# Window attention and a softplus FFN: the order of every engine planned inside the kernel by due times, and the low halves of the weights moved from GpSimd to VectorE

## The chip, the cores and the metric

The kernel runs on one core of one Trainium2 chip. The metric is device time in microseconds (us); lower is better. The engines are TensorE (PE in the profile, PEld its weight loads), VectorE (DVE), ScalarE (ACT), GpSimd (POOL) and SyncE (SP), which issues the DMAs. Each engine runs its own instruction list in order; semaphores tie the lists together.

## The reference

Attention over a window of 64 keys, for 8 batches, 8 heads, 576 tokens and head size 64, and then a feed-forward network (FFN) with a softplus between its two products.

```python
scores = scale * q @ k.T                     # 0 <= row - column < 64 only
attn = exp(scores - max); attn = attn / (sum(attn) + 1e-9)
x = (attn @ v) as 4608 tokens x 512
h = x @ w_in                                 # 512 x 2048
g = maximum(h, 0) + log1p(exp(-abs(h)))
out = g @ w_out                              # 2048 x 512
```

The weights reach the kernel as 64-bit words of double-precision numbers. The kernel makes 32-bit floats of them itself.

## The kernel before

The 4608 tokens are cut into 12 blocks `g` of `TB` = 384. The attention of a block is done in four units `hp` of two heads each (`attention(g, hp)`), so there are 48 units. A unit loads q, k and v, forms scores on PE, takes scaled minima (L258, DVE), exponentials (L295, ACT), scales by the sums (L300, L301, L303, DVE), transposes the result and multiplies by v. It leaves its part of x as two tiles, a rounded high part and the rest (`x0` by ACT, `x1` by DVE, L374 and L375). Blocks 0 and 1 (`by_pe`) transpose on PE (L310) and multiply in 32 bits (L369); block 2 still forms its scores from quarters of the array (`quad`, L268); blocks 3 to 11 use split operands (L281), and blocks 2 to 11 transpose by DMA and multiply in bf16 (L410).

The FFN of a block has 16 steps `f`, one for each 128 columns of the hidden layer; there are 192 steps. `ffn_up(g, f)` (below: U) makes 12 matmuls of 384 columns (L435), then Abs, Exp and Ln on ACT (L439 to L441), the sum on DVE (L443), a rounded copy `g0` (L445, on ACT for blocks 0 and 1 and for odd `f`, else on DVE) and the rest `g1` (L446, DVE). `ffn_down(g, f)` (D) makes 9 matmuls of 512 columns (L456) into three banks of sums. The passes run 8 steps of block 0, 16 of block 1, the other 8 of block 0, and then the blocks 2 to 11 in order. The sums of the first pass are copied out (L475), spilled to DRAM and added later (L473).

`load_w(f)` fetches one of 16 slices of both weight matrices (1 MB of words) and turns it into floats: ACT takes absolute values (L174), DVE does four bit operations (L175 to L178), ACT copies a rounded high part (L181), and GpSimd subtracts it for the low part (L182). Words and half-made floats pass through a few staging tiles (`raws`, `ws`, `raw`, `wh`), which share memory with other things.

The order comes from a list of events with positions written by hand: U of step n at 2n + 0.5, D at 2n + `DOWN` (so D of a step follows the U two steps later), weight slice f at `CONVERT[f]`, and each stage of a unit at `BASE`, `PACE`, `SH`, `SHP` and `STG`. From position `PE_ORDERED_FROM` on (about step 50) PE keeps this order; before that, and on all other engines throughout, the framework's own planner orders the instructions by its timeline.

Of the kernel before, what the change touches and what calls it, by code (L numbers as in the profile page):

```python
# [8 lines left out]
F32 = mybir.dt.float32  # L9
# [12 lines left out]
NCH = TB // CH + 1  # L22

SPLIT = 8
DOWN = 5.5
CONVERT = (-104, -98, -93, -88, -6, -3, 0, 3, 6, 8, 11, 13, 16, 18, 21, 24)
BASE = (-100, -10, 24)
PACE = (5, 4, 7)
STG0 = (-4.5, 0.5, 1, 2, 3, 4, 7, 8)
STG = (-13, -5.9, -5, 0, 1, 2, 3, 4, 5, 6, 7, 7.1, 12, 14, 16, 17)  # L30
SH, SHP = -12, 8
PE_ORDERED_FROM = 100
BY_PE, QUADS = 2, 3
MANUAL = {mybir.EngineType.PE}

ZERO_HIGH = 2.0**-15


@with_exitstack
def window_attention_softplus_ffn(  # L40
# [10 lines left out]

# [21 lines left out]
    ORDER = list(range(0, NT // TB, NPER))[:2]  # L73
    ORDER += [b for b in range(NT // TB) if b not in ORDER]
    QSCALE = -1.0 / float(D) ** 0.5

# [5 lines left out]
    late = ctx.enter_context(tc.tile_pool(name="late", bufs=1))  # L82
# [5 lines left out]
    nc.scalar.preload_act_table_set("natural_log_exp_and_others")  # L88

    NE = NF // 2
    w_first = [[cpool.tile([P, NE, DM], F32R, name=f"w{m}{i}") for i in range(2)] for m in range(2)]
    w_last = {}

    def spare(k, shape, dtype, name):
        return late.tile(shape, dtype, name=name, tag=f"spare{k}")

    def weight(m, i, f):

        if f < NE:
            return w_first[m][i][:, f, :]
        k = (f - NE) // 4
        if (m, i, k) not in w_last:
            w_last[m, i, k] = spare(4 * k + 2 * m + i, [P, 4, DM], F32R, f"w{m}{i}{k}")
        return w_last[m, i, k][:, f % 4, :]


    W = CH + P
# [6 lines left out]
    nc.gpsimd.memset(k_two[:, :, 0:CH], 0.0)  # L116

    v13 = cpool.tile([P, NCH, 2, 2, D], BF16, name="v13")
    nc.gpsimd.memset(v13, 0.0)
    v_first = [att.tile([P, 2, NJ, P], F32, name="v_first", tag=n) for n in ("nat", "tr")]  # L120
    for t in v_first:
        nc.vector.memset(t[0:CH, 0, 0, :], 0.0)

    FAR = BIG / QSCALE
    wide, wide_c, wide_b = [cpool.tile([P, W], BF16, name=n) for n in ("wide", "wide_c", "wide_b")]
    nc.gpsimd.memset(wide, 0.0)
    nc.gpsimd.affine_select(
        out=wide, in_=wide, pattern=[[1, W]], compare_op=ALU.is_gt, fill=FAR, base=0, channel_multiplier=-1  # L130
    )
    nc.gpsimd.affine_select(
        out=wide, in_=wide, pattern=[[-1, W]], compare_op=ALU.is_ge, fill=FAR, base=CH, channel_multiplier=1
    )


    mask_q = att.tile([P, 3, P], BF16, name="mask_q", tag="k0")
    mask, mask_c, mask_b = [mask_q[:, i, :] for i in range(3)]
    for m in (mask_c, mask, mask_b):
        nc.gpsimd.tensor_copy(m[0:CH, :], wide[0:CH, 0:P])  # L140
        nc.gpsimd.tensor_copy(m[CH:P, :], wide[CH:P, CH:W])
    nc.gpsimd.memset(mask_c[0:CH, 0:CH], FAR)
    nc.gpsimd.memset(mask_b[CH:P, 0:CH], FAR)
    nc.gpsimd.tensor_copy(wide_c, wide)
    nc.gpsimd.memset(wide_c[:, 0:CH], FAR)
    nc.gpsimd.tensor_copy(wide_b, wide)
    nc.gpsimd.memset(wide_b[CH:P, 0:P], FAR)
    masks = {True: (mask, mask_c, mask_b), False: (wide, wide_c, wide_b)}
    ident = att.tile([P, P], F32, name="ident", tag="xf")
    make_identity(nc, ident)  # L150

    mm, tp = nc.tensor.matmul, nc.tensor.transpose

    def load_w(f):


        if f < NE + 4:
            k = (0, 4, 2, 6)[f % 4] if f < NE else (4, 6)[f % 2]
            parts = [(spare(k, [P, 2, DM], w_words.dtype, "raws"), spare(k + 1, [P, 2, DM], F32, "ws"), 0, 2)]
        else:  # L160
            parts = [
                (
                    ff.tile([P, 1, DM], w_words.dtype, name="raw"),
                    att.tile([P, 1, DM], F32, name="wh", tag=("v_in", "v12")[m]),
                    m, m + 1,
                )
                for m in range(2)
            ]
        for raw, w, m0, m1 in parts:
            nc.sync.dma_start(raw, w_words[f][:, m0:m1, :])  # L170
            words = raw.bitcast(U32).rearrange("p m (n two) -> p two m n", two=2)
            low, high = words[:, 0, :, :], words[:, 1, :, :]
            wb = w.bitcast(U32)
            nc.scalar.activation(w, high.bitcast(F32), AF.Abs)  # L174
            nc.vector.tensor_scalar(w, w, ZERO_HIGH, None, ALU.max)  # L175
            nc.vector.tensor_scalar(wb, wb, 3, 0x3FFFFFF8, ALU.logical_shift_left, ALU.bitwise_and)  # L176
            nc.vector.scalar_tensor_tensor(wb, high, 0xC0000000, wb, ALU.bitwise_and, ALU.bitwise_or)  # L177
            nc.vector.scalar_tensor_tensor(wb, low, 29, wb, ALU.logical_shift_right, ALU.bitwise_or)  # L178
            for m in range(m0, m1):
                hi, lo = [weight(m, i, f) for i in range(2)]  # L180
                nc.scalar.copy(hi, w[:, m - m0, :])  # L181
                nc.gpsimd.tensor_tensor(lo, w[:, m - m0, :], hi.bitcast(F32), ALU.subtract)  # L182


    xs = {}
    taken_ps = [0]

    def attention(g, hp):
# [3 lines left out]
        by_pe = g < BY_PE  # L192
        quad = g < QUADS
        odd0 = g == 0 and hp % 2 == 1

        def bank():
            if not odd0:
                return ps_a.tile([P, 512], F32, name="ps_a")

            taken_ps[0] += 1  # L200
            return ps_o.tile([P, 512], F32, name=f"ps_o{taken_ps[0] % NJ}")

        heads = [slice(0, D), slice(D, P)]
# [353 lines left out]
```

## Time and profile before

| | |
|---|---|
| median of 3 runs | 1028.54 us (1028.44 to 1029.22) |
| the profiled execution's own time | 1027.8 us |
| its span, first to last instruction | 1026.0 us |
| PE, PEld | 971.5 us (95%), 861.0 us (84%) |
| DVE, ACT, POOL | 796.1 us (78%), 734.9 us (72%), 58.9 us (6%) |
| DMA | 117.38 MB, mean 114 GB/s |

The rows of 40 slices cut the span into stretches of 25.65 us, each digit the busy share in tenths. A group's row gives its line, engine and operation, the busy time, the mean of one instruction, and the idle time ahead of it with what ended most of it. A row of the timeline gives start, length (a merged row's first start to last end), engine, line and count, and in square brackets the idle time before it. The start and end of matmuls are partly modelled.

### The profile page before, as it was taken

How to read it: one execution, taken by the hardware profiler on the slowest of the kernel's cores; microseconds unless marked ns; L12 is line 12 of the kernel's file. 1: busy time of each engine (PE TensorE's matmuls, PEld its weight loads, DVE VectorE, ACT ScalarE, POOL GpSimd, SP SyncE). 2: the span in 40 equal slices, each digit the busy share in tenths (PEclk: the TensorE clock that was granted, in tenths of full speed). 3: DMA queues.
4: the chain of work that ended last, by engine and by line, in shares of the span. 5: the costliest groups of instructions: out<-in, count | busy, mean ns of one | idle time of the engine just before them, and what ended most of it. 6: DMA issues, size and time to landing. Idle time of an engine off the chain costs nothing.

```text
span 1026.0 us, 17028 instructions
## 1 busy us (share of the span) xinstructions
PE 971.5 (95%) x6128; PEld 861.0 (84%) x6128; DVE 796.1 (78%) x1777; ACT 734.9 (72%) x1697; POOL 58.9 (6%) x55
## 2 busy tenths in 40 slices
PE   2668979999999999999999999999999999999998
PEld 2447758888988999898998899899989999888997
DVE  6999585588987888888888878878878887874332
ACT  5556585688877787788778778778778878865443
POOL 4265010000000000000000000000000000000000
PEclk9999989999999999999999999999999999999999
DMA  9653151475553445444444444535645635521000
GB/s 347 214 167 104 40 161 37 83 188 122 142 123 96 113 119 128 114 113 128 120 113 119 128 100 116 145 85 119 157 83 114 165 83 113 133 49 32 31 1 31
DMA packets 201749, 117.38 MB, mean 114 GB/s; under 512 B 130496, under 2 KB 193728, under 8 KB 200128
## 3 DMA queue, kind: packets, MB, share of 16 engines
q1 hardware_dynamic: 201664, 116.29, 43.6%
q8 instruction: 48, 0.79, 0.3%
q14 instruction: 37, 0.30, 0.1%
HBM read 74.58 MB, written 10.22 MB: 83 GB/s over the span
## 4 chain that ended last, share of the span: by engine, by line
PE 84%; DVE 10%; DMA 3%; issue 2%; ACT 1%; SPq 0%; ACTq 0%; DVEq 0%
PE ps_h L435 37%; PE ps_o L456 37%; PE ps_a L410 5%; PE ps_a L281 5%; DVE ws L177 1%; DVE ws L178 1%; DVE st L258 1%; DVE ws L176 1%; DVE st L303 1%; DVE ws L175 1%; DMA raws<-in_w_words_dram 1%; DMA tr<-nat 1%; DVE u L443 1%; DMA raw<-in_w_words_dram 0%; PE ps_a L268 0%
## 5 line engine op out<-in xcount | busy, mean ns | idle before, releaser
L435 PE MATMUL ps_h<-x,w 128*128 128x384 f32 x2304 | 448.5, 342 | 15.3 <-DVE x L375 9.1
L456 PE MATMUL ps_o<-w,g 128*128 128x512 f32 x1728 | 434.5, 394 | 0.5 <-DVE g L446 0.5
L435 PEld LDWEIGHTS ps_h<-x,w 128*128 128x128 f32 x2304 | 405.6, 190 | 31.0 <-DVE x L375 10.8
L456 PEld LDWEIGHTS ps_o<-w,g 128*128 128x128 f32 x1728 | 318.2, 188 | 58.8 <-DVE g L446 1.3
L439 ACT ACTIVATE u<-ps_h 128x384 f32<-128x384 f32 x192 | 94.0, 490 | 129.2 <-PE ps_h L435 126.5
L443 DVE SCALAR_TENSOR_TENSOR u<-ps_h,u 128x384 f32<-128x384 f32 x192 | 106.2, 553 | 75.6 <-ACT u L441 74.3
L295 ACT ACTIVATE st<-st,mn 128x128 f32<-128x128 f32 x288 | 112.1, 390 | 18.4 <-DVE mn L258 14.5
L446 DVE TENSOR_TENSOR g<-u,g 128x384 fp32r<-128x384 f32 x192 | 109.1, 568 | 13.0 <-ACT g L445 11.1
L440 ACT ACTIVATE u<-u 128x384 f32<-128x384 f32 x192 | 100.9, 526 | 3.3
L441 ACT ACTIVATE u<-u 128x384 f32<-128x384 f32 x192 | 100.3, 522 | 4.1
L258 DVE CUSTOM_DVE_ANT_0 st<-ps_a,wide 128x192 f32<-128x192 f32 x176 | 57.0, 351 | 44.5 <-PE ps_a L281 44.4
L410 PEld LDWEIGHTS <-v 128*128 128x128 bf16 x1136 | 56.5, 98 | 21.6 <-issue 20.3
L445 ACT CAST g<-u 128x384 fp32r<-128x384 f32 x112 | 57.0, 509 | 21.1 <-DVE u L443 20.3
L410 PE MATMUL ps_a<-tr,v 128*128 128x128 bf16 (+1 forms) x1136 | 70.2, 211 | 0.2 <-DMA tr<-nat 0.2
L281 PE MATMUL ps_a<-k,q_hl 128*128 128x192 f32 x432 | 69.1, 281 | 0.0
L281 PEld LDWEIGHTS ps_a<-k,q_hl 128*128 128x128 f32 x432 | 59.8, 191 | 3.1
L326 ACT CAST nat<-st 128x768 bf16<-128x768 f32 x40 | 33.2, 830 | 40.0 <-DVE st L324 39.9
L295 ACT ACTIVATION_READ_ACCUMULATOR st<-st,mn 128x1 f32 x288 | 53.9, 187 | 0.0
L415 ACT COPY xf<-ps_a 64x384 f32<-64x384 f32 x80 | 38.1, 477 | 20.2 <-PE ps_a L410 18.9
L303 DVE TENSOR_TENSOR st<-st,sm 128x768 f32<-128x768 f32 x48 | 50.2, 1045 | 1.2
L345 DVE TENSOR_TENSOR v_in<-v_in,v 128x896 f32<-128x896 f32 x40 | 43.5, 1087 | 5.8 <-ACT v L344 5.7
L348 DVE TENSOR_TENSOR v<-v_in,v 64x896 bf16<-64x896 f32 x40 | 43.6, 1089 | 5.1 <-PE ps_a L410 2.1
(81 smaller groups left out, 860.6 us busy)
## 6 DMA issues: line engine op xcount, KB each, us to landing
v_in<-in_v_dram SPq DMA_DIRECT2D x80, 224.0 KB, 3.6
k_in<-in_kT_dram SPq DMA_DIRECT2D x72, 224.0 KB, 3.8
q_in<-in_qT_dram SPq DMA_DIRECT2D x72, 192.0 KB, 4.1
raws<-in_w_words_dram SPq DMA_DIRECT2D x12, 1024.0 KB, 5.7
out_dram<-raw SPq DMA_DIRECT2D x12, 512.0 KB, 2.8
raw<-in_w_words_dram SPq DMA_DIRECT2D x8, 512.0 KB, 5.3
out_dram<-raw SPq DMA_DIRECT2D x12, 256.0 KB, 2.6
q_two<-in_qT_dram SPq DMA_DIRECT2D x12, 192.0 KB, 3.5
```

Source lines behind the costliest of these rows:

```text
L258: nc.vector.tensor_tensor_reduce(st[:, hh, j, :], scores, m, QSCALE, 3.0e38, ALU.add, ALU.min, mn[:, hh, j : j + 1])
L281: mm(spv[:, hh, :], q_hl[:, hh, js], part[:, hh, kc], start=(hh == 0 and i == 0), stop=(hh == 1 and i == 1), skip_group_check=True,)
L295: nc.scalar.activation(sv[:, i, 0:P], sv[:, i, 0:P], AF.Exp, bias=mn[:, hh, j : j + 1], scale=-1.0, accum_out=sm[:, i : i + 1])
L303: nc.vector.tensor_tensor(pn, pn, sm.unsqueeze(2).to_broadcast([P, 2 * NJ, P]), ALU.mult)
L410: mm(av[:, osl], (v13 if s else v12)[:, c, hh, :, :], src, start=(i == 0), stop=(i == len(passes) - 1), skip_group_check=True,)
L435: mm(hv, weight(0, a, f)[:, c * P : (c + 1) * P], x[b][c], start=(i_mm == 0), stop=(i_mm == 3 * NC - 1))
L439: nc.scalar.activation(u, hv, AF.Abs)
L440: nc.scalar.activation(u, u, AF.Exp, scale=-1.0)
L441: nc.scalar.activation(u, u, AF.Ln, bias=1.0)
L443: nc.vector.scalar_tensor_tensor(gf, hv, 0.0, u, ALU.max, ALU.add)
L446: nc.vector.tensor_tensor(gt[1], gf, gt[0].bitcast(F32), ALU.subtract)
L456: mm(ops[g][j], gt[a][:, js], weight(1, b, f), start=(first and i == 0), stop=(last and i == 2),)
```

## The change

The events, their positions and the framework's ordering go. The kernel first writes its work as a list of `Op`s: an engine, a cost in us, the ops that it depends on, and the buffers that it opens or uses. `arrange` then runs these through a small model: on each engine, among the ops that could start, the one with the earliest due time is taken; an op that opens a buffer waits until the buffer's former users are done; a result reaches the next engine `RESULT` later. Due times come from `dues`: U of step n at the time given for it, D at `DOWN` later, a unit's x ahead of its block's first step by `AHEAD` and `APART`, and everything before these by its cost and latency, times `STRETCH`. Four rounds are planned, each with the U times of the last; the one that ends first in the model is emitted, and all engines keep that order (`manual_schedule()` without a list of engines). A DMA's op starts at most `EARLY` before it is due.

In the kernel's work itself: the low part of the weights is subtracted by DVE over both matrices at once, and GpSimd's part goes; each slice has a place of its own (`w{f}`), into which its words land by one DMA and which then takes the floats; copies of block 0 and 1's transposes are all on ACT; six small mask copies go from GpSimd to DVE; q and k have four places instead of two in blocks 0 and 1, and the k of the first two units is issued by ACT; v of blocks 0 and 1 is loaded for all heads at once; the score tiles have three places, the transposed ones two; unit 2 of block 0 uses the banks of U.

```diff
-DOWN = 5.5
-CONVERT = (-104, -98, -93, -88, -6, -3, 0, 3, 6, 8, 11, 13, 16, 18, 21, 24)
...
+DOWN = 6.3
+AHEAD = (1, 1, 8, 8)
+APART = (4, 6, 18, 19)
+STRETCH = 1.4
+EARLY = 30
+RESULT = {"PE": 0.25, "DVE": 0.12, "ACT": 0.15, "POOL": 0.2, "SP": 2.0}
...
+def arrange(ops, rings):
...
+    free = {"PE": 0.0, "DVE": 0.8, "ACT": 2.1, "POOL": 0.8, "SP": 0.8}
...
+    while len(order) < len(ops):
...
+                at = max(ready_at[id(o)], o.due - EARLY if e == "SP" else 0.0)
...
+            t = max(free[e], min(at for at, _ in could))
+            o = min((o for at, o in could if at <= t + 1e-9), key=lambda o: o.due)
+            if best is None or t < best[0]:
+                best = (t, o)
...
-                hi, lo = [weight(m, i, f) for i in range(2)]
-                nc.scalar.copy(hi, w[:, m - m0, :])
-                nc.gpsimd.tensor_tensor(lo, w[:, m - m0, :], hi.bitcast(F32), ALU.subtract)
...
+    w_raw = [buf(cpool, [P, 2, DM], w_words.dtype, "raw", tag=f"w{f}") for f in range(NF)]
+    w_all = [buf(cpool, [P, 2, 2, DM], F32R, "w", tag=f"w{f}") for f in range(NF)]
...
+        a = add("SP", 0.45, lambda: nc.sync.dma_start(raw(), w_words[f]), opens=[raw], nbytes=1024 * 1024, name=f"load{f}")
+        a = add("ACT", 1.05, lambda: nc.scalar.activation(work(), word(1).bitcast(F32), AF.Abs), deps=[a], opens=[work], uses=[raw], name=f"abs{f}")
+        a = add("DVE", 0.6, lambda: ts(work(), work(), ZERO_HIGH, None, ALU.max), deps=[a], uses=[work], name=f"c1.{f}")
...
+        h = add("ACT", 1.05, lambda: nc.scalar.copy(weights(0, f), work()), deps=[a], opens=[w], uses=[work], name=f"hi{f}")
+        lo = add("DVE", 1.13, lambda: tt(weights(1, f), work(), weights(0, f).bitcast(F32), ALU.subtract),
+                 deps=[h], uses=[work, w], name=f"lo{f}")
...
+                if skip:
+                    nc.gpsimd.memset(qk(1)[:, 0:CH], 0.0)
+                by.dma_start(qk(1)[:, skip:], kT[c0 : c0 + P, t0 - CH + skip : t0 + TB])
...
+        a = add("PE", 2.09, up, deps=[o for hp in range(NP) for o in x_ops[g, hp]] + converted[f] + ups[-1:], opens=[hps],
+                uses=[b for i in range(2) for b in x[i]] + [w_all[f]], name=f"U{g}.{f}")
+        s = add("ACT", 1.21, soft, deps=[a], opens=[u], uses=[hps], name=f"soft{g}.{f}")
+        m = add("DVE", 0.47, lambda: stt(u(), hps()[:, :TB], 0.0, u(), ALU.max, ALU.add), deps=[s], uses=[hps, u], name=f"m{g}.{f}")
+        h = add("ACT" if by_act else "DVE", 0.41 if by_act else 0.28,
...
+        lo = add("DVE", 0.47, lambda: tt(gt[1](), u(), gt[0]().bitcast(F32), ALU.subtract), deps=[h], opens=[gt[1]],
+                 uses=[u, gt[0]], name=f"g1.{g}.{f}")
...
+        d = add("PE", 2.06, down, deps=[h, lo, *downs[-1:]], opens=acc if first else [], uses=[*gt, w_all[f]] + ([] if first else acc), name=f"D{g}.{f}")
...
+        for n, t in enumerate(times):
+            ups[n].due = t
+            downs[n].due = t + DOWN
...
+            x1.due = firsts[g] - AHEAD[min(g, 3)] - (NP - 1 - hp) * APART[min(g, 3)]
...
-    for at, emit in events:
-        if at < PE_ORDERED_FROM:
-            emit()
-    with tc.manual_schedule(engines=MANUAL):
...
+    for _ in range(ROUNDS):
...
+        dues(times)
+        order = arrange(ops, rings)
+        end = max(o.end for o in order)
+        if best is None or end < best[0]:
+            best = (end, [(o, o.start) for o in order])
+        times = [o.start for o in ups]
+    with tc.manual_schedule():
+        setup()
+        for o, at in best[1]:
+            o.fn()
```

More of the change, by code (lines that the diff above doesn't have):

```diff
@@ new lines, with __init__, __call__ @@
+EARLY = 30
+ZERO_HIGH = 2.0**-15
+RESULT = {"PE": 0.25, "DVE": 0.12, "ACT": 0.15, "POOL": 0.2, "SP": 2.0}
+BYTES_PER_US = 260e3
+SMALL = 400e3
+class Ring:
+    def __init__(self, n):
+        self.n, self.taken, self.held, self.made = n, [], [], 0
+class Buf:
+    def __init__(self, ring, make):
+        self.ring, self.make, self.tile, self.users = ring, make, None, []
+    def __call__(self):
+        if self.tile is None:
+            self.tile = self.make()
+        return self.tile
+class Op:
+    def __init__(self, eng, cost, fn, deps=(), opens=(), uses=(), nbytes=0, name=""):
+        self.eng, self.cost, self.fn, self.name, self.nbytes = eng, cost, fn, name, nbytes
+        self.deps, self.opens = [d for d in deps if d is not None], list(opens)
+        self.due = self.start = self.end = 0.0
+        self.later = []
+        for d in self.deps:
+            d.later.append(self)
+        for b in [*uses, *opens]:
+            b.users.append(self)
@@ new lines, in attention, with turn @@
+            v_now, lv = v_loads[g]
+            pt = buf(att, [P, 2, TB], F32, "pt", tag=("q_hl", "k1")[hp % 2])
+            cp, t = [], None
+            for hh in range(2):
+                pp = bank()
+                def turn(hh=hh, pp=pp):
+                    for j in range(NJ):
+                        tp(pp()[:, j * P : (j + 1) * P], sv()[:, hh * NJ + j, 0:P], ident)
+                t = add("PE", 0.7, turn, deps=[nrm, t], opens=[pp] if hh else [pp, pt], uses=[st, two["xf"]], name=f"T{tag}")
+                cp.append(add("ACT", 0.4, lambda hh=hh, pp=pp: nc.scalar.copy(pt()[:, hh, :], pp()[:, :TB]),
+                              deps=[t], uses=[pp, pt], name=f"cp{tag}"))
@@ L505, in window_attention_softplus_ffn, with dues @@
-    events.sort(key=lambda e: e[0])
-    for at, emit in events:
-        if at < PE_ORDERED_FROM:
-            emit()
-    with tc.manual_schedule(engines=MANUAL):
-        for at, emit in events:
-            if at >= PE_ORDERED_FROM:
-                emit()
+            attention(g, hp)
+    for n, step in enumerate(steps):
+        ffn(n, *step)
+    def dues(times):
+        for o in ops:
+            o.due = 1e9
+        for n, t in enumerate(times):
+            ups[n].due = t
+            downs[n].due = t + DOWN
+        for n, o in stores:
+            o.due = times[n] + DOWN + 4
+        firsts = {}
+        for n, (g, f, first, last) in enumerate(steps):
+            firsts.setdefault(g, times[n])
+        for (g, hp), (x0, x1) in x_ops.items():
+            x1.due = firsts[g] - AHEAD[min(g, 3)] - (NP - 1 - hp) * APART[min(g, 3)]
+        for o in reversed(topo):
+            for s in o.later:
+                o.due = min(o.due, s.due - STRETCH * (o.cost + RESULT[o.eng]) if s not in downs_set else s.due - o.cost - RESULT[o.eng])
@@ new lines, in window_attention_softplus_ffn @@
+    topo, seen = [], {}
+    for o in ops:
+        seen[id(o)] = len(o.deps)
+    ready = [o for o in ops if not o.deps]
+    while ready:
+        o = ready.pop()
+        topo.append(o)
+        for s in o.later:
+            seen[id(s)] -= 1
+            if not seen[id(s)]:
+                ready.append(s)
+    downs_set = set(downs)
+    times, t = [], 20.0
+    for n, (g, f, first, last) in enumerate(steps):
+        times.append(t)
+        t += 4.2 + (0.6 if g >= 2 else 1.0)
+    best = None
```

735 lines of the change are left out of this document (406 added, 329 removed).

## The prediction

> **What bounds the kernel now.** I read the page's parts 1, 2 and 4 first, then a table of windows, then the timeline of PE and DVE in the first 175 us, and last the waits behind the FFN's chain.
>
> ```profile
> span 1026.0 us, 17028 instructions
> PE   2668979999999999999999999999999999999998
> GB/s 347 214 167 104 40 161 37 83 188 122 142 123 96 113 119 128 114 113 128 120 113 119 128 100 116 145 85 119 157 83 114 165 83 113 133 49 32 31 1 31
> PE 84%; DVE 10%; DMA 3%; issue 2%; ACT 1%; SPq 0%; ACTq 0%; DVEq 0%
> ```
>
> The chain that ended last is PE's. After some seven slices of 25.65 us PE has no idle tenth. The windows say where the border lies:
>
> ```profile
> 30.00:60.00 30.00, 17.41 (x116) 12.61 (x116) 30.00 (x58) 15.85 (x44) 12.72 (x8) 1.00 0.57 194
> 60.00:90.00 30.00, 23.16 (x136) 18.50 (x136) 29.88 (x50) 19.54 (x47) 14.65 (x10) 1.00 0.48 161
> 90.00:126.00 36.00, 32.43 (x234) 27.22 (x234) 26.54 (x60) 22.08 (x61) 12.26 (x8) 1.00 0.12 36
> 126.00:175.00 49.00, 40.59 (x268) 34.83 (x267) 35.42 (x90) 33.81 (x90) 6.14 (x4) 0.93 0.38 112
> 360.85:439.38 78.53, 78.53 (x497) 70.77 (x497) 65.82 (x151) 61.58 (x142) 0.00 (x0) 1.00 0.46 118
> ```
>
> The columns are the stretch, its length, and the busy time of PE, PEld, DVE, ACT and POOL. From 30 to 90 us DVE has no gap. In the last row, one period of the steady part (16 steps and 4 units: 16 x 21 + 4 x 40 = 496 matmuls), PE has none. The price of a step without attention comes from the chain near the end, in order of time:
>
> ```profile
> 927.94 2.10 PE ps_h L435 x12
> 930.05 2.08 PE ps_o L456 x9
> 932.13 2.10 PE ps_h L435 x12
> ```
>
> A step costs PE 932.13 - 927.94 = 4.19 us, and a unit (78.53 - 16 x 4.19)/4 = 2.87 us. All 192 steps are 804.5 us, 36 units of blocks 3 to 11 103.3 us; for block 2's four units I estimate 2.3 us each and for the eight by PE 2.45 us (the rows below). That is 937 us of work at full pace. The kernel needs 1021 us to its last matmul, so about 84 us go to waits and to slow matmuls, and the steady part holds none of them. So the change can gain only in the first 175 us, and it can lose anywhere in the 850 us behind, where there is nothing to gain.
>
> **What the first 175 us are spent on.**
>
> ```profile
> L182 POOL TENSOR_TENSOR w<-ws,w x24: 1273/1720/2327, 16.5 to 99.0; 128x512 fp32r<-128x512 f32 x24
> 124.98 0.69 DVE L475 COPY raw<-ps_o 128x512 f32<-128x512 f32 x1 [1.73 <-PE ps_o L456]
>   DVE x L375: 19.8, 7
> ```
>
> The first row: the subtractions of 12 slices of weights (two rows each) are done by 100 us. The second is the copy of the sums after the first 8 steps: these end at 125 us and need 8 slices. The third, from the list of what L435 waited for: U waited 19.8 us for x. DVE, full as it is, converts weights that are wanted 50 us later while x is late. A planner that goes by due times would turn that around.
>
> **The DVE account to step 8.** Rows of single instructions (minimum/median/maximum in ns):
>
> ```profile
> L175 DVE TENSOR_SCALAR ws<-ws x12: 647/680/1560, 9.5 to 88.9; 128x1024 f32<-128x1024 f32 x12
> L176 DVE TENSOR_SCALAR ws<-ws x12: 676/694/1757, 10.2 to 90.3; 128x1024 uint32<-128x1024 uint32 x12
> L177 DVE SCALAR_TENSOR_TENSOR ws<-raws,ws x12: 1209/1215/2169, 10.9 to 92.5; 128x1024 uint32<-128x1024 uint32 x12
> L178 DVE SCALAR_TENSOR_TENSOR ws<-raws,ws x12: 1209/1212/2290, 13.3 to 95.8; 128x1024 uint32<-128x1024 uint32 x12
> L303 DVE TENSOR_TENSOR st<-st,sm x48: 940/958/2047, 19.3 to 916.2; 128x768 f32<-128x768 f32 x48
> L446 DVE TENSOR_TENSOR g<-u,g x192: 540/551/1648, 83.3 to 1018.1; 128x384 fp32r<-128x384 f32 x192
> 39.02 0.28 DVE L258 CUSTOM_DVE_ANT_0 st<-ps_o,mask_q 128x128 f32<-128x128 f32 x1
> 39.23 0.28 DVE L258 CUSTOM_DVE_ANT_0 st<-ps_o,mask_q 128x128 f32<-128x128 f32 x1
> L375 DVE TENSOR_TENSOR x<-ps_a,x x6: 515/545/558, 31.9 to 128.3; 128x384 fp32r<-128x384 f32 x6
> ```
>
> A slice's four operations are 0.68 + 0.69 + 1.22 + 1.21 = 3.80 us. The moved subtraction (1024 columns of floats, two inputs) has no row on DVE. Its bounds are L303's 0.96 us for 768 columns and L178's maximum of 2.29 us; I take L178's median, 1.21 us, the same width. So a slice costs DVE 5.0 us. What speaks for the move is the maxima: during POOL's subtractions L176 took up to 1.76 us instead of 0.69, L446 1.65 instead of 0.55. With POOL silent these delays go, up to about 1.1 us for each of its 32 subtractions, and 16 x 1.21 = 19 us come in their place. So DVE's sum changes little either way; the account below uses prices without delays.
>
> To the end of step 8, DVE must do 8 slices (40 us), 8 units (six minima at 39.23 - 39.02 = 0.21 us, two small ones of 0.35 together, 0.96 and 0.55: 3.1 us each, 25 us) and 8 FFN steps at 2 x 0.55 (9 us): 74 us. The start:
>
> ```profile
> 3.77 1.56 PE L268 MATMUL ps_a<-k_two,q_two 64*64 64x128 f32 x24 [3.77 <-POOL wide L132]
> 8.34 1.12 ACT L174 ACTIVATE ws<-raws 128x1024 f32<-128x1024 f32 x1 [6.31 <-DMA raws<-in_w_words_dram]
> 15.30 7.55 SPq L170 DMA_DIRECT2D raws<-in_w_words_dram  x2
> ```
>
> The words land at 8.34 us and DVE has weight work from 9.5 us. Until then it can do at most two units' minima (2.5 us) and the six mask copies that leave POOL (about 1 us, hidden there). 9.5 + 74 - 2.5 = 81, a closing D 2 us, and I allow 4 us for gaps: step 8 ends at 87 us instead of 125. The words don't bound this: at the 347 and 214 GB/s of the page's first two columns 1 MB lands each 3 to 5 us, and with a place per slice of weights SP need not sit 7.55 us in two issues (the third row), behind which v waited. The two k issues moved to ACT fall in its idle 6.3 us. The memsets of k stand behind POOL's setup, so the first scores come some 1 to 4 us later than now (3.77 us, the first row); DVE's weight work from 9.5 us covers that, and without this cover it comes out of the allowance. V's 20 loads made 5 only free SP.
>
> **ACT's account to step 8.**
>
> ```profile
> L181 ACT CAST w<-ws x24: 602/618/625, 15.7 to 97.9; 128x512 fp32r<-128x512 f32 x24
> L295 ACT ACTIVATE st<-st,mn x27: 385/386/402, 12.4 to 57.6; 128x128 f32<-128x128 f32 x27
> L311 ACT COPY pt<-ps_a 128x384 f32<-128x384 f32 x6 | 2.8, 475 | 7.3 <-PE ps_a L310 7.3
> ```
>
> A slice costs ACT 1.12 + 2 x 0.62 = 2.4 us, a unit six exponentials of 0.39, two transposes' copies (one came from DVE) and one of x at 0.48: 3.8 us. With some 2.1 us for a step's four operations (rows below) that is 66 us for 8 of each, under DVE's 74.
>
> **The sum.** The state of the kernel before at 175 us, U and D:
>
> ```profile
> L435 PE MATMUL ps_h<-x,w x216: 331/337/689, 29.8 to 174.1; 128*128 128x384 f32 x108
> L456 PE MATMUL ps_o<-w,g x139: 387/393/500, 83.8 to 175.0; 128*128 128x512 f32 x139
> ```
>
> From step 8, PE has 184 steps (771 us), 36 units (103 us), block 2's units (9 us), less the U of the next step, done by then: 881 us. Check on the kernel before: some 18 U (12 matmuls each) and 15.6 D (9 each) are begun by 175 us, and the same prices for the rest give 846 us, so 1021, where its matmuls end. 87 + 881 = 968. The kernel before had step 8 at 125 us, 125 + 881 = 1006, so it lost 15 us more on the way to block 3 (8.4 us of them idle in the row 126:175). In the new kernel that may be anything from 0 to 15; I take 8. Then the steady part, the largest unknown.
>
> **The steady part's new waits.** The FFN chain after a U, near the end where nothing is in its way:
>
> ```profile
> 1004.67 2.27 PE L435 MATMUL ps_h<-x,w 128*128 128x384 f32 x12
> 1006.98 0.49 ACT L439 ACTIVATE u<-ps_h 128x384 f32<-128x384 f32 x1 [2.58 <-PE ps_h L435]
> 1008.61 0.56 DVE L443 SCALAR_TENSOR_TENSOR u<-ps_h,u 128x384 f32<-128x384 f32 x1 [2.50 <-ACT u L441]
> 1009.21 0.51 ACT L445 CAST g<-u 128x384 fp32r<-128x384 f32 x1 [0.63 <-DVE u L443]
> 1009.75 0.56 DVE L446 TENSOR_TENSOR g<-u,g 128x384 fp32r<-128x384 f32 x1 [0.58 <-ACT g L445]
> 1015.15 6.32 PE L456 MATMUL ps_o<-w,g 128*128 128x512 f32 x27
> ```
>
> From U's start to `g1` it takes 1010.31 - 1004.67 = 5.64 us. The planner's costs and latencies make it 2.09 + 0.25 + 1.21 + 0.15 + 0.47 + 0.12 + 0.41 + 0.15 + 0.47 + 0.12 = 5.44 us with the copy on ACT, and 5.04 us with it on DVE: 0.2 and 0.6 us too little, 0.4 on average, mostly because it prices the three ACT operations at 1.21 where 1008.61 - 1006.98 = 1.63 us pass. The old order set D two U's later, 1015.15 - 1004.67 = 10.5 us after the start of its own U. With `DOWN` = 6.3 the due times put it after the next U, at 6.3 us: room of 0.6 us, on an ACT that is busy 61.6 and a DVE that is busy 65.8 of 78.5 us. Where the model sees D late it sends another U first, which brings the old room back. Where it sees it just in time, the chip is late, and behind a late D the whole of PE waits. Bounds: 0 (the model always finds room), and 0.4 us in each of some 160 steps with attention beside them, 64 us. I take a wait of 0.25 us in a third of them, 14 us, nearer to zero since after each wait the other engines have caught up. At the very end the last D comes 2.09 us after its U instead of 6.3, so PE waits 5.64 - 4.19 = 1.5 us.
>
> 968 + 8 + 14 + 1.5 to the last matmul, and 4.5 us of copies and stores as now (1026.0 - 1021.5): a span of 996 us. The profiled execution took 1.8 us more than its span (1027.8), and the median of the runs shown 0.7 more than that: 998 us.
>
> **A slower PE at the start.** Here the same 12 matmuls early and later:
>
> ```profile
> 36.84 1.54 PE L268 MATMUL ps_o<-k_two,q_two 64*64 64x128 f32 x12
> 110.55 0.87 PE L268 MATMUL ps_a<-k_two,q_two 64*64 64x128 f32 x12
> ```
>
> PE works at 0.56 of its pace until about 80 us although the granted clock reads 1.00. If that stays so to step 8, a step costs 4.19 x 1.77 = 7.4 us and a unit 4.3: from a first U at 28 us (four units on ACT, 15 us, behind the first q and k, and a slice) 8 x 7.4 + 4 x 4.3 = 76 us, step 8 at 104. I take DVE's 87, since PE would then be busy without gaps. [...]
>
> **Rivals.** (1) Slower: the FFN chain is late for D in nearly every step. At 64 us instead of 14 the span is 1046, the time 1048. It turns slower from (14 + 1026 - 996)/160 = 0.28 us a step. For it: the model's missing 0.4 us. Against it: the model's own way out, a U ahead. (2) Cold PE binds the first 8 steps, step 8 at 104: 1015 us. For it the rows above, against it DVE's longer account in the gaps. (3) The planned order does no more than the old one in the first part, since DVE's sum is about the same: step 8 at 125, the old 15 us after it and no new waits: 1028. Against it: 12 slices done by 100 us and U waiting for x. (4) No new waits in the steady part: 984 us; a case of my forecast's lower end.
>
> **How the numbers follow.** Forecast with (4): 0.64; its own range 976 to 1012. (2) 0.15; (3) or a like cancelling 0.04; slower by (1) 0.17. Some 0.2% (2 us) is what a measurement here can tell. Faster is 0.64 + 0.15 = 0.79, same 0.04, slower 0.17. The range runs from 976 (0.06 lie below) to 1034, short of (1)'s full price, with 0.12 above.
>
> **What would show it.** Right: POOL's L182 gone, a DVE subtraction of about 1.2 us, L175 to L178 without maxima over 1.4 us; the first full U near 28 us, the spill's copies near 87 instead of 125; PE's idle time behind block 2 about 15 us, ended by `g1`. Wrong: waits of D over 44 us in sum, spread over all blocks, or matmuls at half pace up to 100 us.

## The result and the profile after

The changed kernel takes 995.53 us (median of 4 runs, 993.75 to 995.96) against 1028.49 us before: a ratio of 0.9676, 95% interval 0.9659 to 0.9693. The forecast was 998.0 us, with a range from 976 to 1034. First the page of the changed kernel: its span, the rows of PE, of the granted clock and of the DMA rate over 40 slices, and the chain that ended last.

```profile
span 991.9 us, 16876 instructions
PE   4888998999999999999999999999999999999997
PEclk7899998999999999999999999999999999999999
GB/s 353 241 1 237 220 54 102 151 169 108 113 133 120 86 112 139 122 101 134 104 120 126 127 88 142 109 120 128 110 103 118 137 101 102 148 55 32 33 1 33
PE 69%; ACT 16%; DVE 11%; issue 3%; DMA 1%; POOL 0%; SPq 0%; ACTq 0%; POOLq 0%; DVEq 0%
```

PE is at eight tenths or more from the second slice on. The chain is no longer PE's alone: ACT and DVE hold 27% of it. The third slice has almost no DMA traffic (1 GB/s). The same windows as before (stretch, length, then busy PE, PEld, DVE, ACT, POOL, granted clock, DMA share, GB/s):

```profile
30.00:60.00 30.00, 27.20 (x178) 22.96 (x175) 29.79 (x51) 23.42 (x46) 0.00 (x0) 0.97 0.33 128
60.00:90.00 30.00, 25.41 (x244) 20.18 (x243) 20.35 (x65) 21.09 (x65) 0.00 (x0) 1.00 0.24 85
125.00:175.00 50.00, 43.28 (x326) 37.10 (x325) 47.52 (x101) 39.71 (x90) 0.00 (x0) 0.93 0.35 78
225.00:880.00 655.00, 649.39 (x4067) 583.17 (x4066) 553.55 (x1243) 518.29 (x1169) 0.00 (x0) 1.00 0.49 116
```

From 30 to 90 us PE is busy 52.6 us instead of 40.6. DVE has a third of 60 to 90 free, and is all but full from 125 to 175, where PE stands idle for 6.7 us. Single instructions of VectorE (minimum/median/maximum in ns):

```profile
L250 DVE TENSOR_SCALAR work<-work x16: 679/689/701, 17.3 to 148.6; 128x1024 uint32<-128x1024 uint32 x16
L252 DVE SCALAR_TENSOR_TENSOR work<-raw,work x16: 1210/1224/1233, 18.0 to 150.4; 128x1024 uint32<-128x1024 uint32 x16
L257 DVE TENSOR_TENSOR w<-work,w x16: 1211/1218/1232, 26.1 to 158.1; 128x1024 fp32r<-128x1024 f32 x16
```

The subtraction (L257) costs 1.218 us; the delays of the bit operations are gone. The timeline of PE, of DVE for the spill's copy (L633), and of SP for the first words issued after it (L247):

```profile
5.20 1.56 PE L319 MATMUL ps_a<-k_two,q_two 64*64 64x128 f32 x24 [5.20 <-POOL k_two L306]
18.96 1.55 PE L450 MATMUL ps_a<-pt,v_two 128*64 128x64 f32 x24 [2.56 <-DMA v_two<-in_v_dram]
30.66 2.54 PE L574 MATMUL ps_h<-x,w 128*128 128x384 f32 x10
36.23 0.89 PE L319 MATMUL ps_a<-k_two,q_two 64*64 64x128 f32 x24
38.94 2.35 PE L574 MATMUL ps_h<-x,w 128*128 128x384 f32 x12 [1.81 <-DVE u L586]
81.50 0.69 DVE L633 COPY raw<-ps_o 128x512 f32<-128x512 f32 x1 [0.69 <-PE ps_o L598]
83.08 0.49 SPq L247 DMA_DIRECT2D raw<-in_w_words_dram  x1
153.43 4.18 PE L574 MATMUL ps_h<-x,w 128*128 128x384 f32 x12 [6.31 <-DVE u L586]
158.61 2.35 PE L598 MATMUL ps_o<-w,g 128*128 128x512 f32 x9
946.74 2.25 PE L574 MATMUL ps_h<-x,w 128*128 128x384 f32 x12
950.89 2.25 PE L574 MATMUL ps_h<-x,w 128*128 128x384 f32 x12
979.93 6.35 PE L598 MATMUL ps_o<-w,g 128*128 128x512 f32 x27
```

The first U starts at 30.66 us, step 8 is done at 81.5 instead of 125. At 153.43 PE had waited 6.31 us for DVE's `u`.

**A ledger.** PE's idle time misses matmuls that are slow or held up by their weight loads (in the steady part of the changed kernel it is 5.6 us where 12.2 are lost, as shown further down). So I count the matmuls of U, of D and of the blocks 2 to 11's attention in a stretch, price them at full pace (a step 950.89 - 946.74 = 4.15 us, a unit 2.87 us as in the prediction), and call the rest of the stretch lost; all of block 0 and 1's attention and of block 2's scores counts as lost, alike in every kernel. The counts by 225 us are these (for before and after; U and D):

```profile
L435 PE MATMUL ps_h<-x,w 128*128 128x384 f32 x336 | 73.2, 364 | 15.3 <-DVE x L375 9.1 <-DVE u L443 5.0 <-ACT x L374 1.1
L456 PE MATMUL ps_o<-w,g 128*128 128x512 f32 x230 | 59.2, 397 | 0.5 <-DVE g L446 0.5
```

```profile
L574 PE MATMUL ps_h<-x,w 128*128 128x384 f32 x438 | 86.3, 347 | 8.9 <-DVE u L586 8.1 <-DVE x L457 0.4 <-DVE w L257 0.4
L598 PE MATMUL ps_o<-w,g 128*128 128x512 f32 x306 | 77.5, 399 | 2.4 <-DVE g L589 1.4 <-ACT g L588 0.9
```

The changed kernel has done 102 matmuls of U and 76 of D more by then, 35 us of work, and some of the next blocks' attention. The ledger for all kernels of this study, in us; the last column is the end of the plan in the kernel's own model:

| kernel | lost before 225 us | lost behind 225 us | span | plan's end |
|---|---|---|---|---|
| before | 106.8 | 13.4 | 1026.0 | |
| after | 67.0 | 19.2 | 991.9 | 979.5 |
| before_lo_on_dve | 102.0 | 13.6 | 1021.2 | |
| lo_on_pool | 83.4 | 8.2 | 997.2 | 973.5 |
| weights_first | 111.0 | 8.4 | 1025.5 | 999.2 |
| few_buffers | 74.7 | 33.9 | 1014.2 | 987.2 |
| conversions_50us_earlier | 86.3 | 10.7 | 1002.6 | 996.9 |
| one_transposed_tile | 71.7 | 17.6 | 995.2 | 988.9 |
| down_4_2 | 64.8 | 11.2 | 982.0 | 982.3 |
| true_softplus_cost | 68.9 | 7.0 | 981.6 | 984.2 |
| early_35 | 66.4 | 7.6 | 980.0 | 978.3 |
| early_35_true_softplus_cost | 61.6 | 7.1 | 974.7 | 978.2 |
| all_measured_costs | 61.6 | 10.1 | 977.6 | 982.9 |
| lo_on_pool_true_cost | 79.5 | 7.1 | 992.7 | 976.7 |

So the change gained 39.8 us before 225 us and gave 5.8 back behind it. (Of the 13.4 us of the kernel before, 4.5 are its tail, the copies and stores behind the last matmul, and most of the rest its pace, 4.19 us a step.)

Each row is one profiled execution, and any edit makes another plan. The six kernels that do the same work and differ only in the planner's numbers (after, down_4_2, true_softplus_cost, early_35, early_35_true_softplus_cost, all_measured_costs) lose 61.6 to 68.9 us before 225 us. So a difference of up to 7 us there is not, by itself, shown to be the effect of an edit.

### The profile page after: what moved, and what is told of

Same layout as the page of the kernel before. It is cut to its first block, busy times and chain, and to the rows that moved or that the text cites. A ratio compares the mean times of both kernels' runs of the same rounds, so it can differ in the third digit from the quotient of the medians.

```text
span 991.9 us, 16876 instructions
## 1 busy us (share of the span) xinstructions
PE 950.3 (96%) x6128; PEld 847.9 (85%) x6128; DVE 796.2 (80%) x1776; ACT 744.8 (75%) x1685; POOL 4.5 (0%) x18
## 4 chain that ended last, share of the span: by engine, by line
PE 69%; ACT 16%; DVE 11%; issue 3%; DMA 1%; POOL 0%; SPq 0%; ACTq 0%; POOLq 0%; DVEq 0%
PE ps_o L598 31%; PE ps_h L574 30%; ACT st L388 4%; PE ps_a L542 3%; PE ps_a L363 3%; ACT u L579 2%; ACT u L578 2%; DVE u L586 1%; ACT xf L549 1%; DVE st L290 1%; ACT v L500 1%; DVE work L252 1%; DVE w L257 1%; ACT k L351 1%; ACT u L580 1%
## 5 line engine op out<-in xcount | busy, mean ns | idle before, releaser
L574 PE MATMUL ps_h<-x,w 128*128 128x384 f32 x2304 | 436.5, 339 | 11.8 <-DVE u L586 10.9
L598 PEld LDWEIGHTS ps_o<-w,g 128*128 128x128 f32 x1728 | 315.0, 188 | 73.8 <-DVE g L589 14.6
L586 DVE SCALAR_TENSOR_TENSOR u<-ps_h,u 128x384 f32<-128x384 f32 x192 | 106.6, 555 | 83.3 <-ACT u L580 81.5
L388 ACT ACTIVATE st<-st,mn 128x128 f32<-128x128 f32 x288 | 111.8, 390 | 19.2 <-DVE st L380 11.7
L589 DVE TENSOR_TENSOR g<-u,g 128x384 fp32r<-128x384 f32 x192 | 106.6, 555 | 13.0 <-ACT g L588 8.4
L290 DVE CUSTOM_DVE_ANT_0 st<-ps_a,wide 128x192 f32<-128x192 f32 x176 | 53.6, 351 | 14.2 <-PE ps_a L363 13.3
L542 PE MATMUL ps_a<-tr,v 128*128 128x128 bf16 (+1 forms) x1136 | 61.5, 211 | 0.0
L363 PE MATMUL ps_a<-k,q_hl 128*128 128x192 f32 x432 | 57.5, 271 | 0.0
L503 DVE TENSOR_TENSOR v<-v_in,v 64x896 bf16<-64x896 f32 x40 | 43.6, 1090 | 13.4 <-ACT v L502 12.8
L351 ACT CAST k<-k_in 128x896 fp32r<-128x896 f32 x36 | 33.6, 934 | 24.6 <-PE ps_a L363 24.2
L502 ACT CAST v<-v_in 128x896 bf16<-128x896 f32 x40 | 37.4, 934 | 16.8 <-DVE v_in L501 16.8
L551 DVE TENSOR_TENSOR xf<-ps_a,xf 64x384 f32<-64x384 f32 x80 | 44.0, 550 | 4.7 <-ACT xf L549 2.5
L403 DVE TENSOR_TENSOR st<-st,sm 128x768 f32<-128x768 f32 x48 | 45.8, 954 | 0.9
## 6 DMA issues: line engine op xcount, KB each, us to landing
raw<-in_w_words_dram SPq DMA_DIRECT2D x16, 1024.0 KB, 12.2
```

Source lines behind the costliest of these rows:

```text
L290: nc.vector.tensor_tensor_reduce(st()[:, hh, j, 0:width], scores, m, QSCALE, 3.0e38, ALU.add, ALU.min, mn()[:, hh, j : j + 1])
L363: mm(spv[:, hh, :], q_hl()[:, hh, j * P : (j + 1) * P], k_s[i]()[:, hh, j * P : j * P + W], start=(hh == 0 and i == 0), stop=(hh == 1 and ...
L388: nc.scalar.activation(sv()[:, i, 0:P], sv()[:, i, 0:P], AF.Exp, bias=mn()[:, hh, j : j + 1], scale=-1.0, accum_out=sm()[:, i : i + 1],)
L542: mm(av()[:, osl], (v3() if s else v12())[:, c, hh, :, :], src, start=(i == 0), stop=(i == len(passes) - 1), skip_group_check=True,)
L574: mm(hps()[:, :TB], weight(0, a, f)[:, c * P : (c + 1) * P], x[b][c](), start=(i_mm == 0), stop=(i_mm == 3 * NC - 1))
L586: m = add("DVE", 0.47, lambda: stt(u(), hps()[:, :TB], 0.0, u(), ALU.max, ALU.add), deps=[s], uses=[hps, u], name=f"m{g}.{f}")
```

## The experiments

**Where the low part is subtracted.** The changed kernel with GpSimd again:

```diff
-        lo = add("DVE", 1.13, lambda: tt(weights(1, f), work(), weights(0, f).bitcast(F32), ALU.subtract), ...
+        def low():
+            for m in range(2):
+                nc.gpsimd.tensor_tensor(weight(1, 1, f) if m else weight(0, 1, f), work()[:, m, :], weight(m, 0, f).bitcast(F32), ALU.subtract)
+        lo = add("POOL", 3.3, low, ...
```

> The changed kernel with one part undone: GpSimd subtracts the low parts again (two subtractions a slice, planned as one op of 3.3 us), everything else planned as before. Order theory (the gain is the planned order; the move to VectorE is about even): VectorE loses 16 x 1.22 = 19 us of work but its operations beside GpSimd's take up to 1.1 us longer, 32 times; the time stays within -6 and +10 us of 995.5. Port theory (the gain is a silent GpSimd): most of the 33 us is lost, 1015 us or more. Load theory (VectorE's load binds the first 160 us, so the 19 us count): about 6 us faster, as the planner's own model says, which knows nothing of delays (its end is 973.5 instead of 979.5 us).

998.68 us, ratio to before 0.9705 (0.9689 to 0.9722): 3 us more than after. And the kernel before with `nc.gpsimd.tensor_tensor(lo, ...)` made `nc.vector.tensor_tensor(lo, ...)`, in the old order:

> The kernel before with one part alone: VectorE subtracts the low parts, in the same 32 halves; the hand-written positions and the framework's ordering stay. Order theory: within 6 us of 1028.5 either way, since 32 x 0.69 = 22 us come onto VectorE and delays of the same size go. Port theory: at least 20 us faster. Load theory: VectorE is full from 30 to 90 us, so up to 10 us slower.

1023.22 us, 0.9946 (0.9931 to 0.9961): 5.3 us less. Taken by the times, the place of the subtraction seemed worth 3 to 5 us, and the theories that gave it more were wrong. The ledger says otherwise for the first: 16.4 us more lost before 225 us, hidden by 11.0 less behind, where its plan happened to have fewer waits. That reading was tested last, on a kernel without those waits (below).

**The order.** Two kernels put the conversions first. One shifts their due times by 50 us and sets `EARLY = 100`; in its plan one k is loaded over a k not yet used, so one unit's scores come from another unit's k, with the same work.

```diff
+        for o in ops:
+            if o.name.startswith(("abs", "c1.", "c2.", "c3.", "c4.", "hi", "lo")) and not o.nbytes:
+                o.due -= 50
```

> The changed kernel with the due times of the weights' conversion (on ScalarE and VectorE) set 50 us earlier, and EARLY raised from 30 to 100 so that the words are there: weights go ahead of x, as in the kernel before. Order theory: x is late again, the first full U comes after 45 us instead of 31, step 8 ends after 95 us instead of 81, and the time rises by 15 to 30 us. Port theory and buffer theory (the gain is a place for each slice and more early buffers): less than 6 us of change, since both are kept.

1027.62 us, 0.9993 (0.9984 to 1.0003): the whole gain is gone, more than was expected. PE waited 33.5 us for minima and 23.6 us for a k behind the words in the queue. The second kernel keeps `EARLY = 30` and plans q and k as one op.

> The changed kernel with the due times of the weight conversions (ScalarE's and VectorE's seven operations of a slice) put 50 us earlier; the loads of the words keep their due times and are still held to at most 30 us before them, so the queue of loads stays as it is. q and k of a unit are planned as one op on SP. Order theory (weights ahead of x cost the time, whatever the DMA queue does): the conversions are taken as soon as their words land, x and the first full U come later than 30.7 us, and the kernel takes 1007 to 1017 us (the plan's own model has 16 to 17 us more than for the changed kernel). DMA theory (what cost the 32 us in the kernel with all weights first was that words crowded q and k out of the queue): k and q land as in the changed kernel, and the time stays within 4 us of 995.5.

1004.38 us, 0.9768 (0.9753 to 0.9782), 9 us more than after: 2.6 us under the interval of the order theory and outside that of the DMA theory. Its timeline shows two reasons why x is late:

```profile
49.86 1.22 DVE L254 SCALAR_TENSOR_TENSOR work<-raw,work 128x1024 uint32<-128x1024 uint32 x1
51.00 0.55 DVE L463 TENSOR_TENSOR x<-ps_a,x 128x384 fp32r<-128x384 f32 x1
29.00 1.56 PE L325 MATMUL ps_a<-k_two,q_two 64*64 64x128 f32 x24 [12.02 <-DMA k_two<-in_kT_dram]
33.48 1.55 PE L456 MATMUL ps_a<-pt,v_two 128*64 128x64 f32 x24 [2.92 <-DMA v_two<-in_v_dram]
52.07 0.90 PE L445 MATMUL ps_o<-ident,st 128*128 128x128 f32 x3 [15.76 <-DVE x L463]
63.72 5.02 PE L580 MATMUL ps_h<-x,w 128*128 128x384 f32 x24
```

Weight operations stand back to back on DVE, and x comes behind them: PE waits 15.76 us for it. But the queue was not as in the changed kernel either. SP issued seven slices' words in a row from 4.35 us, so a k landed late, and the first product with v began at 33.48 us, when v had landed, instead of at 18.96. The first U starts 33 us later than in the changed kernel, the loss before 225 us is 19.3 us larger, and this run does not separate the two reasons. In weights_first it is 44.0 us larger; the rest of that may be the queue's words, the larger `EARLY` or the plan, which no run has alone.

**The early buffers.** Two places for q and k, two score tiles, two of `mn` and `sm`, one transposed tile, unit 2 not in U's banks:

```diff
-            slot = held("qk", qk_slots) if g < 2 else held("qk_near", qk_slots[:2])
+            slot = held("qk_near", qk_slots[:2])
...
-        st = held("st_quad", st_quad) if quad else ...
+        st = held("st_quad", st_quad[:2]) if quad else ...
...
-            pt = buf(att, [P, 2, TB], F32, "pt", tag=("q_hl", "k1")[hp % 2])
+            pt = buf(att, [P, 2, TB], F32, "pt", tag="q_hl")
```

In this plan three units' k are loaded over ones not yet used (the op of k does not open the place), so the two places hold for q alone and three units' scores come from another unit's k; the work is the same.

> The changed kernel with the early buffers as before: q and k of blocks 0 and 1 have two places instead of four, the score tiles and their minima and sums two instead of three, the transposed scores one instead of two, and unit 2 of block 0 uses the attention's banks instead of the U's. Weights keep a place each. Order theory: 3 to 10 us slower, since x of block 0 waits for places (first full U some 5 us later). Buffer theory: more than half of the 33 us lost, 1012 us or more.

1016.21 us, 0.9875 (0.9861 to 0.989), 20.7 us more than after. By the time alone the buffers had won. The ledger takes that back: 7.7 us more are lost before 225 us, 14.7 more behind it. There PE's weight loads waited (in us, times, longest; the same list of the changed kernel stands further down):

```profile
PEld ps_o L598 <- DVE g L589: 20.0, 43, 0.9
PEld ps_o L598 <- DVE g L588: 7.2, 14, 0.8
```

One transposed tile by itself (the last line of the diff):

> The changed kernel with one place for the transposed scores (pt) instead of two; all other early buffers stay. If this buffer is what the kernel with few buffers lacked (its chain showed waits of 7.2 and 4.1 us for pt), x of blocks 0 and 1 comes later by some us per unit, the first full U near 40 us, and the time is 1005 to 1013 us (the plan's own model has 9 us more than for the changed kernel). If it was the two places of q and k (waits of 6.9 and 3.1 us there), this kernel stays within 4 us of 995.5.

996.95 us, 0.9698 (0.9682 to 0.9714): within the 4 us of the rival, so by the time the wait for `pt` was not what the kernel with few buffers lacked. The ledger is less sure: 4.7 us more are lost before 225 us, of the 7.7 with few buffers. Both are within the 7 us by which plans differ, so which of the early buffers counts, and how much, stays open.

**The room of D and the planner's costs.** Three numbers were moved: `DOWN`, the cost of the softplus, and `EARLY` (with it the number of planning rounds).

> The changed kernel with DOWN = 4.2 instead of 6.3: D is due one step (4.2 us) after its U instead of one and a half, less than the 5.64 us that the chain from U to g1 takes. If room of D is what limits the steady part, TensorE's idle time between 225 and 880 us rises from 5.6 us to 20 us or more, with D waiting for g1, and the time is 1005 to 1030 us. If the model finds the room anyway (it sends another U first whenever D is not ready), idle time in that stretch stays under 12 us and the time is 994 to 1003 us.

987.31 us, 0.9595 (0.9574 to 0.9616): 8 us faster than after, 2.0 us of idle PE from 225 to 880. (Its four runs spread from 983.8 to 988.9 us; the ledger shows the fastest.) The first theory is wrong: the smaller `DOWN` made D's weight loads wait only 2.3 us for `g1` from 225 us on, presumably since the plan finds another U; and the time lies under the second's interval, too.

```diff
-EARLY = 30
+EARLY = 35
-ROUNDS = 4
+ROUNDS = 8
...
-        s = add("ACT", 1.21, soft, deps=[a], opens=[u], uses=[hps], name=f"soft{g}.{f}")
+        s = add("ACT", 1.63, soft, deps=[a], opens=[u], uses=[hps], name=f"soft{g}.{f}")
```

> The changed kernel with ScalarE's three softplus operations planned at the 1.63 us that the trace shows instead of 1.21, loads allowed 35 us before they are due instead of 30, and eight rounds of planning instead of four. Theory of late conversions (the 24 us lost between step 8 and the steady part come from slices that are loaded and converted too late, while VectorE stands idle 5 to 10 us of each 30 between 60 and 100 us): earlier words and a truer model bring 3 to 8 us, 988 to 993 us, and VectorE is busier before 100 us. Rival (those losses are the noise of a plan: any new plan loses about as much elsewhere): 993 to 1000 us. In the steady part (225 to 880 us) the truer cost leaves less than the 5.6 us of idle TensorE time.

976.3 us, 0.9492 (0.9478 to 0.9506): 19 us faster than after and more than either theory gave. Each part alone:

> The changed kernel with one number altered: the planner's cost of ScalarE's three softplus operations 1.63 us instead of 1.21 (EARLY 30 and four rounds as they were). The kernel with this cost, EARLY 35 and eight rounds took 976.3 us. Theory of the missing 0.4 us: a plan that sees the true length of the chain from U to g1 has no waits for it on the chip, and most of the 19 us come from this number: 977 to 985 us, under 1 us of idle TensorE time from 225 to 880 us, and no wait for u over 4 us in 90 to 180 us, although the plan's own model ends 5 us later than that of the changed kernel. Rival, earlier words: 990 us or more here, and the kernel with EARLY 35 alone takes the gain. Rival, the model's end decides: 998 to 1002 us.

> The changed kernel with EARLY 35 instead of 30 and eight rounds of planning instead of four, the softplus cost left at 1.21 us. Theory of the missing 0.4 us: waits for u and g stay, 4 us or more of idle TensorE time from 225 to 880 us, and the time is 990 to 1000 us. Rival, earlier words: 976 to 984 us. The plan's own model ends 1.2 us earlier than that of the changed kernel.

984.55 us, 0.957 (0.9555 to 0.9584), and 981.66 us, 0.9536 (0.952 to 0.9552). For the cost, the first theory's time and its signs came out; for `EARLY`, the time of the rival, but not for the rival's reason. Alone, it did not bring the first late words earlier (SP issued them at 84.29 us, against 83.08 in the changed kernel), and by the ledger 0.6 us of its gain lie before 225 us and 11.6 behind. Its eight rounds do nothing here: in the planner's model the second round's plan ends first. With both numbers it is the sixth round's, so there the rounds are a third difference. What PE's weight loads waited for in the steady part, after (first two lines) and with both numbers moved (the longest line of its list):

```profile
PEld ps_o L598 <- DVE g L589: 10.4, 27, 1.0
PEld ps_h L574 <- DVE u L586: 5.7, 8, 0.8
```

```profile
PEld L542 <- issue: 6.6, 30, 0.3
```

With the true cost, alone or with `EARLY`, no weight load of U or D waits for `g` or `u`. With that number alone 7.0 us are lost behind 225 us, 5.4 of them its tail; the tail of after is 5.6 (991.9 - 979.93 - 6.35). So the waits of the steady part cost the changed kernel some 12.2 us. But `early_35` keeps the cost of 1.21 and loses only 7.6 there, against its expectation. The short cost makes late D's possible, not certain: with it the eight plans lose 7.6 to 33.9 us behind 225 us, the four with 1.63 lose 7.0 to 10.1.

In the first 225 us neither number alone changes much (68.9 and 66.4 against 67.0), both together gain 5.4, which is within the 7 us by which plans differ. U waited there for `w`, a late slice, 7.5 us with the true cost alone, 2.6 with `EARLY` alone and 1.2 with both, and for `u` 3.7, 6.5 and 3.4 us. One more kernel has the true cost, the conversions' measured durations, `STRETCH` 1.7 instead of 1.4 and `DOWN` 5.3 instead of 6.3, all at `EARLY = 30`:

> The changed kernel with the softplus cost of 1.63 us, the weight conversion's seven operations at the durations of the trace as well (ScalarE 1.13 instead of 1.05, VectorE 0.68 instead of 0.60 and 1.22 instead of 1.13), STRETCH 1.7 instead of 1.4 and DOWN 5.3 instead of 6.3; EARLY 30 and four rounds. If truer costs in the planner are what counts, the conversions' too: 972 to 980 us, with less idle TensorE time from 90 to 175 us than in the kernel of 976.3 us (1.4 us there). If VectorE's and ScalarE's durations in the trace are longer than the spacing at which they issue, so that the planner's figures were right for all but the softplus: 978 to 988 us, since the conversions are then planned too slow.

979.44 us, 0.9519 (0.9504 to 0.9533), 0.2 us of waits for `w` and the same 61.6 us before 225. The time lies in both intervals, and PE's idle time from 90 to 175 us is 4.5 us, not under 1.4. So truer costs of the conversions are not shown to be better than the other two numbers, and with so many numbers moved at once this run isolates none.

**The place again, with the better plan.** The kernel of 976.3 us with the subtractions on GpSimd, by the first diff:

> The kernel of 976.3 us (softplus cost 1.63 us, EARLY 35, eight rounds) with GpSimd subtracting the low parts again, two halves of 1.7 us per slice, planned as one op of 3.3 us. The first such kernel took 3 us more than the changed kernel, but by the work that TensorE had done it lost 16 us more before 225 us and 11 us less behind, where its plan had fewer waits of D for g1. Theory that the place of the subtraction is worth about 16 us in the first part (GpSimd's operations hold up VectorE, maxima of 1.8 and 2.3 us in the conversions instead of 0.7 and 1.2, and the longer chain of a slice): with the steady part free of waits in both kernels, this one takes 986 to 996 us, and step 8 or the conversions are later. Rival (the place is worth nothing, the 16 us were that plan's): 974 to 981 us; the plan's own model ends 1.5 us earlier than that of the kernel of 976.3 us.

994.46 us, 0.9667 (0.9651 to 0.9683): 18 us more, all of them before 225 us (79.5 against 61.6), behind it 7.1 in both. Groups of DVE up to 225 us (busy us, mean ns), first with GpSimd:

```profile
L592 DVE TENSOR_TENSOR g<-u,g 128x384 fp32r<-128x384 f32 x33 | 24.2, 734 | 1.6 <-ACT g L591 1.2
L252 DVE SCALAR_TENSOR_TENSOR work<-raw,work 128x1024 uint32<-128x1024 uint32 x16 | 23.4, 1465 | 0.4
L589 DVE SCALAR_TENSOR_TENSOR u<-ps_h,u 128x384 f32<-128x384 f32 x33 | 18.1, 552 | 10.7 <-ACT u L583 10.4
```

and in the kernel of 976.3 us:

```profile
L589 DVE TENSOR_TENSOR g<-u,g 128x384 fp32r<-128x384 f32 x36 | 19.8, 551 | 0.7 <-ACT g L588 0.6
L586 DVE SCALAR_TENSOR_TENSOR u<-ps_h,u 128x384 f32<-128x384 f32 x36 | 19.8, 550 | 5.5 <-ACT u L580 5.2
L252 DVE SCALAR_TENSOR_TENSOR work<-raw,work 128x1024 uint32<-128x1024 uint32 x16 | 19.5, 1221 | 0.3
```

Beside GpSimd `g1` takes 734 ns instead of 551 on average, the bit operation 1465 instead of 1221, while `m` (the sum on DVE, `u<-ps_h,u`) stays at 552 against 550. An operation with a single input was held up as well: L250 took up to 1644 ns, 758 on average against 689 in the kernel of 976.3 us. Why `m` is spared, and by what GpSimd holds the others up, no run shows. DVE's work up to 225 us hardly differs: the four bit operations (L249, L250, L252, L254) take 71.0 us instead of 61.0 and 33 `g1` some 6 us more, where the other kernel's subtractions (L257) are 19.5 us, so delays stand in place of subtractions. The waits do differ: U waited 12.0 us for `u` and D 6.4 us for `g` before 225 us, against 3.4 and 0.6. That the plan does not know of the delays, and that a slice has a longer chain (two subtractions of 1.79 us on GpSimd instead of one of 1.22 on DVE), are both possible causes; no run tells them apart. That the place itself is worth 16 to 18 us before 225 us shows on two pairs of plans (83.4 against 67.0, 79.5 against 61.6), well over their scatter.

## Why the prediction was right

**The start and the first eight steps.** Predicted: first U near 28, step 8 at 87 us. Measured: 30.66 and 81.5. DVE's account (5.0 us a slice, the subtraction at 1.21) held: 1.218 us, no maxima over 1.4 us. Up to 81.5 us DVE had done just the 8 slices, 8 units (but for two units' x) and 8 steps of the account and was busy 72.7 us, against 74 predicted. The weight work began at 16.6 us, not at 9.5, but the minima of the units stood ahead of it. DVE's sum over the whole kernel stayed (796.2 against 796.1). The first scores came at 5.2 us instead of 3.77, within the 1 to 4 us allowed.

**Order or place.** The prediction credited the order and held the place to be neutral by DVE's sum. The sum was right, the conclusion was not: in the planned order the place is worth 16 to 18 us, in the old one 5. For the order, compare what DVE did up to the end of step 8, before (to 124.98 us) and after (to 81.5 us):

```profile
L177 DVE SCALAR_TENSOR_TENSOR ws<-raws,ws 128x1024 uint32<-128x1024 uint32 x12 | 17.3, 1440 | 0.0
L177 DVE SCALAR_TENSOR_TENSOR wh<-raw,wh 128x512 uint32<-128x512 uint32 x4 | 3.1, 795 | 0.0
```

```profile
L252 DVE SCALAR_TENSOR_TENSOR work<-raw,work 128x1024 uint32<-128x1024 uint32 x8 | 9.8, 1219 | 0.1
```

The kernel before had put the bit operations of 14 slices (12 whole and four halves) ahead of step 8, the changed one those of 8. All rows of these four operations come to 69.1 us before and 30.5 after, where the eight subtractions add 9.7. At the undelayed 3.80 us a slice, the six slices that were not wanted yet are 23 us, which is the order; the other 16 are delays, which belong to the place: L177 takes up to 2169 ns before, and the same operation (L252) up to 2199 in lo_on_pool but at most 1233 in the changed kernel, where GpSimd's subtractions are gone. Undone alone, by the ledger, the place costs 16 to 18 us, the conversions put first 19 (the late k and v in it), and the few buffers 8, which is hardly over the scatter; they overlap within the 39.8.

**The way to block 3.** Predicted 8 us, within 0 to 15. From step 8 at 81.5 us and 881 us of work, the last matmul should come at 962.5 without further waits; it came at 986.3. Of these 24 us 12.2 are the steady part's, so about 12 remain here; 2 of them are the next U, which the prediction took as done by then and which was not. The largest single one is the row at 153.43. DVE had worked on late slices and the next blocks' attention there, with `m` behind them, while from 60 to 90 us it had 9.6 us free and DMA moved 85 GB/s. In the plan `EARLY` held these words back (the ninth slice's load starts at 87.7 us, 30 before it is due); on the chip SP issued the first of them at 83.08 us, behind the store of the spill, as the plan has it. The prediction did not see this wait; its size fell inside the bound.

**The steady part.** Predicted 14 us of waits ended by `g1`; 12.2 measured by the ledger, ended by `g1` and, for a third, by `u`. PE's own idle time shows only 5.6; the rest stands in the waits of the weight loads. The reason given, a softplus planned 0.4 us too short, was right in that the two plans with the true cost and the other costs as they were have none of it (all_measured_costs has 1.6 us, for `u`), but not a necessity, as `early_35` shows.

**The end.** The 1.5 us for the last D did not come: 27 matmuls of D stand in one row at 979.93, as before.

**What was luck.** The forecast is 2.5 us off, closer than its terms. Step 8 came 5.5 us earlier than predicted, the way to block 3 took about 4 us longer, the steady part and the end 3 us less, and the pace of 4.15 us a step (last section) hides a part of the longer way. That the place is worth time stood in no term of its own, though the account to step 8 has it, by its durations without delays.

**The rivals.** (1) The slower case would have needed 0.28 us a step; 12.2 us over 160 steps are 0.08. (2) A slow PE to step 8: false. The 24 matmuls of a unit's scores take 1.56 us at 5.20 and 0.89 at 36.23, so the full pace is there at 36 us, after dense work since 26.3 us (PE busy 9.5 of 9.9 us). (The row of before at 110.55 has 12 of them, in 0.87 us; its row at 36.84 has 12, too.) At 153.43 the U behind 6.31 us of idle time took 4.18 us instead of the 2.35 at 38.94, and the next D at 158.61 was again at 2.35. The slow row of before at 36.84 stands among many gaps (PE busy 17.4 of 30 us there); that they are its cause is the author's estimate and was not tested. (3) and (4): the first part gained 39.8 us, and the steady waits were there, but not needed: the kernels without them reach 976 to 985 us.

## What to carry to other kernels

Judge a replanned kernel by work done up to a border and behind it, not by its time alone: twice here a loss in the first part was hidden or swollen by waits behind 225 us at which the edit was not aimed. And compare with the scatter of plans that do the same work, here 7 us, before an edit is given the credit. Give a planner the measured length of a dependent chain (1.63 us, not 1.21) and look at what weight loads wait for; PE's idle time showed less than half of it here (5.6 of 12.2 us). The subtractions moved off the busy VectorE to GpSimd took 19.5 us from it up to 225 us and brought it delays of 16 there, and the move cost 18 us.

## What was not expected of the hardware

The same 21 matmuls of a step did not take the same time everywhere: 4.19 us before (927.94 to 932.13), 4.15 in after. At 0.04 us each, all 192 steps would make 8 us, a part of the gain that the prediction, which took 4.19 for both, did not have; the 12 us of the way to block 3 are reckoned with 4.19 and would be up to 8 larger at after's own pace. In all_measured_costs a step took 4.21 us at the end (934.38 - 930.17). The granted clock reads 1.00 before and after (920 to 960 us), and no run isolates the cause.
